# A fused attention and feed-forward layer on one core: half of two chunks' attention spreads issued by GpSimd, one score half added in pairs on VectorE, a second norm without scaled row sums, and a new instruction order

## The chip, the cores and the metric

The kernel runs on one core of a Trainium2 chip. The metric is the device time of one execution in microseconds (us); lower is better. Engine names are those of the profile: PE is TensorE (matmuls), PEld its weight loads, DVE is VectorE, ACT is ScalarE, POOL is GpSimd, SP is SyncE, which here only issues transfers (DMAs). A name with a q at its end (SPq, ACTq, POOLq) is the instruction stream of that engine that issues transfers.

## The reference

Input x has 2048 rows of 512 in bf16. One layer is computed: a norm, sliding attention, a residual, a second norm, a gated feed-forward part, a second residual.

```python
x = A_x
h = x + A(layernorm(x), wqkv, wo)
h2 = h + B(layernorm(h), W_gate, W_up, W_down)

# A: 32 heads of 16; each position looks at 8 keys, 2 apart, backwards
idx = pos[:, None] - arange(8) * 2
logits = einsum("bhsd,bhswd->bhsw", q, k[idx]) * 16 ** -0.5   # masked where idx < 0
o = einsum("bhsw,bhswd->bhsd", softmax(logits), v[idx])       # then o @ wo

# B: 512 -> 1376 -> 512
out = (relu(x @ W_gate) * (x @ W_up)) @ W_down
```

## The kernel before, in words

The 2048 rows are worked on in four chunks of 512, numbered 0 to 3. In a chunk:

1. **Norm and projections.** DVE takes the statistics of x (L469, L472), ACT or DVE centres and scales it (L514, L517), PE or a transposing DMA turns it (L546, L535). Twelve groups of four matmuls make q, k and v (L587; chunk 0's are cut in short pieces that follow the first weights and rows as they come), and ACT copies each from its PSUM bank (L595).
2. **Scores.** The eight keys of a position are two halves of four. For each half, DVE multiplies q by four shifted views of k: two products of 128x4096 for two pairs of feature groups (L638; for chunk 0 four products of 128x2048, L653). PE sums the features of each head by sixteen matmuls with a 0/1 matrix `sel` (L644). For the chunk halves in a list `PRE`, DVE first adds the two products (L682), and PE has only eight matmuls (L689). ACT takes the exponential (L703), and chunk 0's is masked by DVE (L706).
3. **Softmax and spread.** The two halves are added (L735), PE sums over the keys (L720), ACT makes the reciprocal (L726, L729), and DVE multiplies (L747; for chunk 0 only at the end, L802). Each half of the weights is then spread by four DMAs over the 16 features of each head (L763, `big<-ex` in the profile, 128 KB each). A table `BCD` has a letter for each of the four: S for SP's queue, P for POOL's.
4. **Weighted sum.** DVE multiplies the spread weights by v (L795; chunk 0 L810), and the eight products are added: the first step, eight to four, mostly by an accumulating DMA from POOL (L838, 512 KB), the rest by DVE (L798, L802, L832).
5. **Output projection and residual.** PE multiplies by wo, four groups of four matmuls (L876). DVE adds x and sums each row (L887).
6. **Second norm.** DVE multiplies each row sum by -1/512 (L452). ACT takes the sum of squares of x less the mean (L458). DVE centres x (L512). The rows aren't scaled here; the inverse variance is applied to the output of the feed-forward part.
7. **Feed-forward.** Pairs of 128 columns: PE makes up and gate (L949; the last 96 columns L916), ACT evacuates them (L953, L956) into two buffers each, DVE multiplies (L977, L926). Then PE multiplies by W_down (L1000), in groups of the first eight and the last three column blocks.
8. **Output.** DVE scales and adds the residual (L1008; chunks 0 and 1 by ACT and an accumulating DMA, L1006, L1029), and a DMA writes it (L1014, L1032). The last row block of chunk 3 is cut in pieces of 256, 128 and 128 columns.

Nothing fixes the order but a planner: the steps are gathered as operations, and a table of ranks, `RANK`, one number for each in the order of gathering, says in which order they are given out. Each engine then works through its own stream in that order and waits where an input, or a buffer to write to, isn't there. PE has eight PSUM banks; the 4096-wide tiles have six places (`big`, one of them the space of wqk_sb when its weights are done with). Ahead of the plan stands `setup`, which issues the first loads from SP's and ACT's queues, in a fixed order.

Of the kernel before, what the change touches and what calls it, by code (L numbers as in the profile page):

```python
# [8 lines left out]
P = 128  # L9
BF16 = mybir.dt.bfloat16  # L10
F32 = mybir.dt.float32
I32 = mybir.dt.int32
ACT = mybir.ActivationFunctionType
ALU = mybir.AluOpType
# [187 lines left out]
def kernel(  # L202
# [19 lines left out]
    DIL = 2  # L222
    PADL = 16
    DEN1 = (0, 1, 2, 3)
    BCD = {(0,0):"SSSS",(0,1):"SSSS",(1,0):"SSSS",(1,1):"SSSS",(2,0):"SSSS",(2,1):"SSSS",(3,0):"SSSS",(3,1):"SSSS"}
    PRE = ((3,0),(3,1))
    PRD = ()
    ODA = (0, 1)
# [861 lines left out]
```

## Time and profile before

| what | us |
|---|---|
| time, median of 3 runs | 192.63 (192.53 to 192.71) |
| the profiled execution, its time | 193.22 |
| its span, from the first to the last instruction | 191.3 |
| PE busy | 185.3 |
| DVE busy | 149.6 |
| ACT busy | 115.2 |
| POOL busy | 18.5 |

The span is the part of the profiled execution that the trace shows. The rest of its time, 1.9 us, lies around it. The profiled execution is 0.59 us longer than the median of the three runs. The mean granted clock of TensorE was 0.997.

In rows by time, the first number is the start, the second the length, and an idle time with what ended it stands in square brackets. In rows by group there is after the bar the busy time, the mean length of one in ns, and the idle time ahead of them. In rows of DMA issues the last number is the median time from issue to landing. Instructions of a group overlap at their ends, so that the step from one to the next is shorter than their length.

### The profile page before, as it was taken

To read this page: it belongs to the slowest core of one execution; us is meant where nothing else is said; L and a number is where in the kernel's file an instruction comes from. 1 tells how busy PE (TensorE), PEld (TensorE's weight loads), DVE (VectorE), ACT (ScalarE), POOL (GpSimd) and SP (SyncE) were. 2 spreads that over 40 slices of the span, in tenths; PEclk is the share of its full clock that TensorE was granted. 3 is DMA by queue.
4 is the path that set the end of the run, shared out by engine and by line. 5 is a ranking of instruction groups with operands and counts; after the bars stand their busy time and mean duration, and the time that the engine had idled before them with its cause. 6 is when DMAs were issued, how large, how long until landed. Compare 5 with 4: busy or idle time off the path is not lost.

```text
span 191.3 us, 3033 instructions
## 1 busy us (share of the span) xinstructions
PE 185.3 (97%) x1101; PEld 96.5 (50%) x1120; DVE 149.6 (78%) x246; ACT 115.2 (60%) x236; POOL 18.5 (10%) x34
## 2 busy tenths in 40 slices
PE   7899999999999999999999999999999999999993
PEld 7795555544455444644445544444446444445452
DVE  6899999999999999999999987999627503212632
ACT  2589999976748967753454875144855528517500
POOL 3000002500000042000055000042100000000000
PEclk9999999999999999999999999999999999999998
DMA  5998464992068589993479916779900460120302
GB/s 159 331 351 327 102 157 84 200 196 45 0 258 228 168 154 193 183 279 61 88 131 186 203 33 139 164 151 186 211 4 0 82 165 0 31 82 0 82 25 88
DMA packets 26718, 26.44 MB, mean 138 GB/s; under 512 B 12528, under 2 KB 22608, under 8 KB 26704
## 3 DMA queue, kind: packets, MB, share of 16 engines
q1 hardware_dynamic: 23248, 16.39, 30.9%
q0 software_dynamic: 2736, 8.91, 25.1%
q10 hardware_dynamic: 720, 0.95, 1.5%
q8 instruction: 9, 0.15, 0.3%
q14 instruction: 5, 0.04, 0.1%
HBM read 8.42 MB, written 2.10 MB: 55 GB/s over the span
## 4 chain that ended last, share of the span: by engine, by line
PE 94%; DMA 3%; issue 1%; ACTq 0%; DVE 0%
PE bank L949 36%; PE bank L587 22%; PE bank L1000 20%; PE bank L876 7%; DMA wqk_sb<-in_A_wqkv_dram 3%; PE bank L644 3%; PE bank L916 3%; PE bank L546 2%; PE bank L689 1%; PE bank L720 0%; ACTq L324 0%; ACTq L322 0%; DVE row L1008 0%
## 5 line engine op out<-in xcount | busy, mean ns | idle before, releaser
L949 PE MATMUL bank<-quad,wgu_sb 128*128 128x512 bf16 x311 | 72.1, 379 | 0.4
L949 PEld LDWEIGHTS <-wgu_sb 128*128 128x128 bf16 x320 | 30.9, 98 | 36.9 <-issue 1.7
L1000 PE MATMUL bank<-wd_sb,gT 128*128 128x512 bf16 (+3 forms) x195 | 39.6, 355 | 0.2
L956 ACT ACTIVATE gr<-bank 128x512 bf16<-128x512 f32 x40 | 23.2, 607 | 17.0 <-PE bank L949 13.0
L977 DVE TENSOR_TENSOR gT<-gr,up_sb 128x1024 bf16<-128x1024 bf16 x20 | 13.7, 688 | 23.5 <-ACT up_sb L953 20.3
L587 PE MATMUL bank<-quad,wqk_sb 128*128 128x512 bf16 (+2 forms) x171 | 30.0, 319 | 1.0 <-DMA wqk_sb<-in_A_wqkv_dram 0.7
L953 ACT CAST up_sb<-bank 128x512 bf16<-128x512 f32 x40 | 22.6, 594 | 10.5 <-PE bank L949 8.5
L1000 PEld LDWEIGHTS <-gT 128*128 128x128 bf16 (+1 forms) x198 | 18.5, 98 | 19.9
L638 DVE TENSOR_TENSOR big<-quad,kT 128x4096 bf16<-128x4096 bf16 x11 | 24.9, 2283 | 0.0
L587 PEld LDWEIGHTS <-wqk_sb 128*128 128x128 bf16 x176 | 16.9, 114 | 11.2 <-DMA wqk_sb<-in_A_wqkv_dram 0.9
L795 DVE TENSOR_TENSOR big<-big,vT 128x4096 bf16<-128x4096 bf16 x9 | 20.2, 2282 | 0.0
L458 ACT ACTIVATE junk<-x_sm,mv 128x512 bf16<-128x512 bf16 x16 | 11.7, 730 | 10.0 <-DVE mv L452 9.9
L587 PE MATMUL bank<-quad,wv_sb 128*128 128x512 bf16 x63 | 15.6, 379 | 0.1
L876 PE MATMUL bank<-wo_sb,quad 128*128 128x512 bf16 x63 | 15.2, 379 | 0.1
L838 POOL DMA_DIRECT2D big<-big x12 | 11.2, 1018 | 38.5 <-PE bank L587 29.4
L887 DVE SCALAR_TENSOR_TENSOR x_sm<-x_sm,bank 128x512 bf16<-128x512 bf16 x16 | 10.5, 680 | 3.7 <-PE bank L876 3.7
L798 DVE TENSOR_TENSOR big<-big 128x1024 bf16<-128x1024 bf16 (+2 forms) x18 | 11.5, 655 | 0.1
L1008 DVE SCALAR_TENSOR_TENSOR row<-bank,iv,x_sm 128x512 bf16<-128x512 f32 (+2 forms) x10 | 6.2, 640 | 6.8 <-PE bank L1000 6.8
L469 DVE BATCH_NORM_STATS2 st<-x_sm 128x6 f32<-128x512 bf16 x16 | 10.3, 681 | 1.2 <-DMA x_sm<-in_A_x_dram 1.2
L595 ACT CAST kT<-bank 128x512 bf16<-128x512 f32 x16 | 9.1, 592 | 2.8 <-DVE big L638 2.8
L595 ACT CAST quad<-bank 128x512 bf16<-128x512 f32 x16 | 9.4, 596 | 2.1 <-PE bank L587 1.9
L595 ACT CAST vT<-bank 128x512 bf16<-128x512 f32 x16 | 9.4, 596 | 2.0 <-PE bank L587 2.0
(79 smaller groups left out, 173.7 us busy)
## 6 DMA issues: line engine op xcount, KB each, us to landing
big<-big POOLq DMA_DIRECT2D x12, 512.0 KB, 5.7
big<-ex SPq DMA_DIRECT2D x32, 128.0 KB, 2.7
wqk_sb<-wqk_sb POOLq DMA_DIRECT2D x3, 512.0 KB, 4.5
wgu_sb<-in_B_W_gate_dram SPq DMA_DIRECT2D x1, 1376.0 KB, 11.2
wgu_sb<-in_B_W_up_dram SPq DMA_DIRECT2D x2, 688.0 KB, 4.7
wd_sb<-in_B_W_down_dram SPq DMA_DIRECT2D x2, 640.0 KB, 5.2
x_sm<-in_A_x_dram SPq DMA_DIRECT2D x2, 512.0 KB, 7.2
x_sm<-up_sb POOLq DMA_DIRECT2D x4, 256.0 KB, 5.1
```

What stands on the lines that cost most here:

```text
L458: nc.scalar.activation(out=junk[:, j % 2, :], in_=h.t[:] if h else x_sm[:, tk * BPC + j, :], func=ACT.Square, bias=mv.t[:, j, 0:1], scale= ...
L587: nc.tensor.matmul(mm.t[:, lo:hi], lhsT=wv_sb[:, dt, t:D:NT] if c == 2 else wqk_sb[:, dt, c * D + t:(c + 1) * D:NT], rhs=xnT.t[:, dt, lo:h ...
L595: nc.scalar.copy(out=o, in_=mm.t[:])
L638: V.tensor_tensor(out=pb.t[:].rearrange("p (t w) s -> p t w s", t=2), in0=q4, in1=k4, op=ALU.mult)
L795: V.tensor_tensor(out=mt.t[:], in0=ab.t[:], in1=v8, op=ALU.mult)
L798: V.tensor_tensor(out=mt.t[:, 0:n, :], in0=mt.t[:, 0:n, :], in1=mt.t[:, n:2 * n, :], op=ALU.add)
L876: nc.tensor.matmul(od.t[:], lhsT=OT.t[:, t, j * P:(j + 1) * P], rhs=wo_sb[:, t, :], start=(t == 0), stop=(t == NT - 1 and tk not in RPE))
L949: nc.tensor.matmul(mm.t[:fs, lo:hi], lhsT=wgu_sb[:, dt, g, ft * P: ft * P + fs], rhs=hnT.t[:, dt, lo:hi], start=(dt == 0), stop=(dt == NT ...
L953: nc.scalar.copy(out=ub.t[:fs, i, :], in_=um.t[:fs, :])
L956: nc.scalar.activation(out=gr.t[:fs, i, :], in_=gm.t[:fs, :], func=ACT.Relu)
L977: V.tensor_tensor(out=gt.t[:fs, 0:n, :], in0=gr.t[:fs, 0:n, :], in1=ub.t[:fs, 0:n, :], op=ALU.mult)
L1000: nc.tensor.matmul(od.t[:, c0:c1], lhsT=gts[ft].t[:fs, ft % 2, j * P:(j + 1) * P], rhs=wd_sb[:fs, ft, c0:c1], start=(ft == 0), stop=(ft == ...
```

## The change

There are five parts.

- **Spreads.** `BCD` for chunks 0 and 1 goes from "SSSS" to "SSPP": the first two of the four DMAs of each half stay with SP, the last two go to POOL.
- **Scores.** `PRE` gains (2,1): the second half of chunk 2 has its two products added by one 128x4096 addition on DVE, and 8 matmuls in place of 16.
- **Second norm.** The row sums aren't multiplied by -1/512. ACT squares 512 x less the sum instead (the small constant inside the logarithm grows by 512 squared), and DVE's centring becomes 512 x less the sum: two operations in one instruction, with a number and the row sum as operands. The common factor of 512 goes out with the inverse variance.
- **Numbers of the planner.** Estimated durations and latencies are changed. They issue nothing; they set which places and banks are taken.
- **Order.** `RANK` is a new table, so that instructions of all engines stand in other places.

```diff
-                    late = 3.0 if at < free.get("DT", -1.0) + 0.8 else 0.0
+                    late = 3.0 if at < free.get("DT", -1.0) - 0.5 else 0.0
...
-    BCD = {(0,0):"SSSS",(0,1):"SSSS",(1,0):"SSSS",(1,1):"SSSS",(2,0):"SSSS",(2,1):"SSSS",(3,0):"SSSS",(3,1):"SSSS"}
-    PRE = ((3,0),(3,1))
+    BCD = {(0,0):"SSPP",(0,1):"SSPP",(1,0):"SSPP",(1,1):"SSPP",(2,0):"SSSS",(2,1):"SSSS",(3,0):"SSSS",(3,1):"SSSS"}
+    PRE = ((2,1),(3,0),(3,1))
...
-                    def f_nm(j=j):
-                        V.tensor_scalar(out=mv.t[:, j, 0:1], in0=sm.t[:, j:j + 1], scalar1=-1.0 / D,
-                                        scalar2=None, op0=ALU.mult)
...
-                                             bias=mv.t[:, j, 0:1], scale=1.0, accum_out=sq.t[:, j:j + 1])
+                                             bias=sm.t[:, j:j + 1], scale=-float(D), accum_out=sq.t[:, j:j + 1])
...
-                    V.tensor_scalar(out=xn.t[:], in0=x, scalar1=mv.t[:, j, 0:1], scalar2=None, op0=ALU.add)
+                    V.tensor_scalar(out=xn.t[:], in0=x, scalar1=float(D), scalar2=sm.t[:, j:j + 1], op0=ALU.mult, op1=ALU.subtract)
...
-    MM, TP = 0.2165, 0.057
+    MM, TP = 0.2158, 0.056
```

Three places of the order are shown, each before and then now.

**POOL's stream, from the end of the setup on.** `ex` is a half of the softmax weights, `big` a 4096-wide tile; x2 is two instructions. Before, chunk 0's four accumulations stand first, then chunk 1's:

```order
L338 MEMSET wqk_sb 1x1
L838 DMA big_89<-big_89 128x2048
L838 DMA big_88<-big_88 128x2048
L838 DMA big_90<-big_90 128x2048
L838 DMA big_91<-big_91 128x2048
L838 DMA wqk_sb<-wqk_sb 128x2048
```

Now:

```order
L340 MEMSET wqk_sb 1x1
L767 DMA big_92<-ex_100 128x1x512 x2
L767 DMA big_92<-ex_101 128x1x512 x2
L842 DMA big_88<-big_88 128x2048
L842 DMA big_90<-big_90 128x2048
L842 DMA big_89<-big_89 128x2048
L842 DMA big_91<-big_91 128x2048
L767 DMA big_91<-ex_100 128x1x512 x2
L767 DMA big_91<-ex_102 128x1x512 x2
L842 DMA big_89<-big_89 128x2048
```

Two spreads of each half stand ahead of the accumulations of their chunk; in chunk 1 the second half (ex_100) comes first.

**DVE's stream in the middle, from the last products of chunk 2 on.** L638 (now L635) is a product of q and k, L795 (L799) one of the spread weights and v of chunk 1, L977 (L981) a gate product of chunk 0. Before:

```order
L638 TENSOR_TENSOR big_91<-quad_87,kT 128x4096
L638 TENSOR_TENSOR big_89<-quad_87,kT 128x4096
L638 TENSOR_TENSOR big_92<-quad_87,kT 128x4096
L795 TENSOR_TENSOR wqk_sb<-big_88,vT 128x4096
L795 TENSOR_TENSOR big_90<-big_88,vT 128x4096
L795 TENSOR_TENSOR big_91<-big_88,vT 128x4096
L977 TENSOR_TENSOR gT_93<-gr_111,up_sb_109 128x1024
```

Now:

```order
L635 TENSOR_TENSOR big_89<-quad_87,kT 128x4096
L635 TENSOR_TENSOR big_88<-quad_87,kT 128x4096
L635 TENSOR_TENSOR big_90<-quad_87,kT 128x4096
L799 TENSOR_TENSOR wqk_sb<-big_91,vT 128x4096
L799 TENSOR_TENSOR big_89<-big_91,vT 128x4096
L679 TENSOR_TENSOR big_92<-big_92,big_88 128x4096
L799 TENSOR_TENSOR big_90<-big_91,vT 128x4096
L981 TENSOR_TENSOR gT_93<-gr_112,up_sb_109 128x1024
```

The new addition (L679) stands among the products of chunk 1, ahead of the first gate product.

**DVE's stream at the very end.** These are the outputs of chunk 3, each from a PSUM bank to a row buffer. Before:

```order
L1008 SCALAR_TENSOR_TENSOR row_104<-bank_138,iv_136,x_sm 128x256
L1008 SCALAR_TENSOR_TENSOR row_108<-bank_141,iv_136,x_sm 128x512
L1008 SCALAR_TENSOR_TENSOR row_105<-bank_144,iv_136,x_sm 128x512
L1008 SCALAR_TENSOR_TENSOR row_106<-bank_143,iv_136,x_sm 128x512
L1008 SCALAR_TENSOR_TENSOR row_104<-bank_140,iv_136,x_sm 128x128
L1008 SCALAR_TENSOR_TENSOR row_104<-bank_139,iv_136,x_sm 128x128
```

Now:

```order
L1012 SCALAR_TENSOR_TENSOR row_108<-bank_141,iv_136,x_sm 128x512
L1012 SCALAR_TENSOR_TENSOR row_104<-bank_142,iv_136,x_sm 128x128
L1012 SCALAR_TENSOR_TENSOR row_106<-bank_139,iv_136,x_sm 128x512
L1012 SCALAR_TENSOR_TENSOR row_105<-bank_144,iv_136,x_sm 128x512
L1012 SCALAR_TENSOR_TENSOR row_104<-bank_140,iv_136,x_sm 128x256
L1012 SCALAR_TENSOR_TENSOR row_104<-bank_145,iv_136,x_sm 128x128
```

The piece of 256 columns moved from the first place to the last but one, and the last piece is now the one that ACT's queue writes out (columns 384 to 512); before it was the one ahead of it, which SP's queue writes.

More of the change, by code (lines that the diff above doesn't have):

```diff
@@ L445, in layernorm @@
         for grp in groups:
-            ag, nms = [], {}
+            ag = []
             gk = str(grp[0]) if len(groups) > 1 else ""
@@ L459, in f_sq @@
                                              func=ACT.Square,
-                                             bias=mv.t[:, j, 0:1], scale=1.0, accum_out=sq.t[:, j:j + 1])
-                    a = nms[j] = add((ln + "nm" + gk, tk), "DVE", DSM, f_nm, [src[j][0]], pr, take=[mv], use=[sm], lat=DL)
-                    ag.append(add((ln + "sq" + gk, tk), "ACT", 0.66 if h else 0.72, f_sq, [a], pr,
-                                  take=[sq], use=[mv] + ([h] if h else []), lat=AL))
+                                             bias=sm.t[:, j:j + 1], scale=-float(D), accum_out=sq.t[:, j:j + 1])
+                    ag.append(add((ln + "sq" + gk, tk), "ACT", 0.66 if h else 0.72, f_sq, [src[j][0]], pr,
+                                  take=[sq], use=[sm] + ([h] if h else []), lat=AL))
                 else:
@@ L522, in norm @@
                 f = lambda: f_xn(j, xn)
-                d, u = ([nms[j]], [mv]) if residual else ([e], [nb, rs] if on_act else [mv, rs])
+                d, u = ([src[j][0]], [sm]) if residual else ([e], [nb, rs] if on_act else [mv, rs])
                 if on_act:
                     return xn, add((ln + "xn" + gk, tk), "ACT", AX, f, d, pr, take=[xn], use=u, lat=AL)
-                return xn, add((ln + "xn" + gk, tk), "DVE", DXN, f, d, pr, take=[xn], use=u, lat=DL)
+                return xn, add((ln + "xn" + gk, tk), "DVE", 0.27 if residual else DXN, f, d, pr, take=[xn], use=u, lat=DL)
             step = 1 if tk == 0 and not residual else 2
@@ L684, with f_pb, f_sc @@
                 a = add(("pa%d" % hf, tk), "DVE", D40, f_pa, [a for a, _, _ in prd], apr, use=[b for _, b, _ in prd], lat=DL)
-                def f_sc(sc=sc, pb=prd[0][1]):
-                    for u in range(2):
+                nu = 2
+                if (tk, hf) in PRE2:
+                    def f_pb(p0=prd[0][1]):
+                        V.tensor_tensor(out=p0.t[:, 0:4, :], in0=p0.t[:, 0:4, :], in1=p0.t[:, 4:8, :], op=ALU.add)
+                    a = add(("pb%d" % hf, tk), "DVE", D20, f_pb, [a], apr, use=[prd[0][1]], lat=DL)
+                    nu = 1
+                def f_sc(sc=sc, pb=prd[0][1], nu=nu):
+                    for u in range(nu):
                         for g in range(4):
@@ L894 @@
             else:
-                a = add(("rs%d" % j, tk), "DVE", 0.63, f_rs, [a], base + 50, take=[sm], use=[od], lat=DL)
+                a = add(("rs%d" % j, tk), "DVE", 0.613, f_rs, [a], base + 50, take=[sm], use=[od], lat=DL)
             hd.append((a, od))
@@ L1043 @@
         if o.dq and o.eng in ("SP", "ACT"):
-            o.hw = 4 if n[:2] == "bd" else 2 if n == "ldd" and o.dur > 0.5 else 1
+            o.hw = round(o.dur / 0.7) if n[:2] == "bd" else 2 if n == "ldd" and o.dur > 0.5 else 1
         if n in ("qe1", "qe5"):
```

44 lines of the change are left out of this document (23 added, 21 removed), and 74 rows, old and new, of the table RANK.

## The prediction

> **What bounds the kernel now.** I read the page's busy shares and slices first.
>
> ```profile
> PE 185.3 (97%) x1101; PEld 96.5 (50%) x1120; DVE 149.6 (78%) x246; ACT 115.2 (60%) x236; POOL 18.5 (10%) x34
> ...
> PE   7899999999999999999999999999999999999993
> ...
> DVE  6899999999999999999999987999627503212632
> ...
> PE 94%; DMA 3%; issue 1%; ACTq 0%; DVE 0%
> ```
>
> PE is at 9 in every slice from the third to the last but one, and the last row, the chain by engine, is PE for 94%. DVE is at 9 too but for two slices, though only up to the 28th (about 134 us). The windows view says how full that is.
>
> ```profile
> 12.00:62.00 50.00, 49.58 (x330) 26.42 (x335) 49.83 (x79) 41.34 (x76) 3.62 (x4) 1.00 0.65 169
> 62.00:112.00 50.00, 49.74 (x268) 23.43 (x273) 49.15 (x57) 31.62 (x69) 8.70 (x10) 1.00 0.77 161
> 112.00:150.00 38.00, 37.79 (x184) 17.96 (x186) 29.80 (x60) 20.96 (x46) 4.33 (x5) 1.00 0.54 109
> ```
>
> The third column is PE, the fifth DVE. PE lacks 0.4 us in the first 50 and 0.3 us in the next, at a granted clock of 1.00. DVE lacks 0.2 and 0.9 us. So PE sets the end, and DVE runs beside it with almost no room until 112 us. The chain of waits then gives PE's two ends.
>
> ```profile
> 1.67 6.42 DMA wqk_sb<-in_A_wqkv_dram
> ...
> 8.14 0.81 PE bank L587 x11
> ...
> 49.75 0.98 PE bank L644 x16
> ...
> 95.38 0.55 PE bank L689 x8
> ...
> 180.15 8.03 PE bank L1000 x58
> ...
> 188.20 0.35 DVE row L1008
> ```
>
> From 8.14 to 188.18 us PE is without a break: 180.04 us of matmuls. Ahead of it lies the load of wqk_sb, behind it one DVE output and its transfer to 191.3 us. A change here pays only what it takes from these 180.04 us or from the ends; anything that comes late to PE is added.
>
> **What the change takes from PE.** The second score group of chunk 2 goes from 16 matmuls to 8, because the two products are added first. The chain has both forms: 0.98 us for 16 (L644) and 0.55 us for 8 (L689, chunk 3). Gain 0.43 us, in full on the path. No other PE work is removed; everything else is moved.
>
> **What it puts on DVE.** One 4096-wide add is new; sixteen tiny multiplications go; the sixteen centring instructions become two-operation ones.
>
> ```profile
> 91.92 2.28 DVE L682 TENSOR_TENSOR big<-big,wqk_sb 128x4096 bf16<-128x4096 bf16 x1
> 94.12 4.49 DVE L795 TENSOR_TENSOR big<-big,vT 128x4096 bf16<-128x4096 bf16 x2
> ...
> 55.47 0.32 DVE L452 TENSOR_SCALAR mv<-sm 128x1 f32<-128x1 f32 x4
> 55.72 0.41 DVE L747 TENSOR_TENSOR ex<-ex,rec 128x512 bf16<-128x512 bf16 x1
> ...
> L512 DVE TENSOR_SCALAR row<-x_sm,mv 128x512 bf16<-128x512 bf16 x16 | 5.1, 348 | 0.3
> L517 DVE TENSOR_SCALAR row<-x_sm,mv,rs 128x512 bf16<-128x512 bf16 x4 | 1.5, 402 | 0.0
> ```
>
> The add holds DVE from 91.92 to 94.12: 2.20 us. Four row sums take 0.25 us, so sixteen give back 1.0. The new centring is not in the trace. Its bounds are 0 (it costs as L512) and 16 x 0.054 = 0.9 us (as L517, the nearest two-operation row, though with both operands per row); I take 0.4. DVE's net is +1.6 us, of which +2.2 comes at once in chunk 2. Whether that costs anything is read at the places where PE takes what DVE makes.
>
> ```profile
> 49.76 0.76 DVE L802 TENSOR_TENSOR quad<-big,rec 128x512 bf16<-128x512 bf16 x2
> 50.66 2.77 PE L876 MATMUL bank<-wo_sb,quad 128*128 128x512 bf16 x12
> ...
> 84.54 0.69 DVE L977 TENSOR_TENSOR gT<-gr,up_sb 128x1024 bf16<-128x1024 bf16 x1
> 85.70 1.03 PE L1000 MATMUL bank<-wd_sb,gT 128*128 128x512 bf16 x4
> ```
>
> *Chunk 0's output projection.* Before, DVE ends its last input at 50.52 and PE starts at 50.66: 0.14 us to spare. In the new order one 4096-wide product of chunk 1 stands behind these instructions instead of ahead: 50.52 - 2.20 = 48.32. PE has a score group (0.98) and, net, one projection of four matmuls (0.86) less ahead: 50.66 - 1.84 = 48.82. To spare: 0.50 us.
>
> *Chunk 0's down projection.* Before, the last of the first four gate products ends at 85.23 and PE starts at 85.70. In the new order DVE has the add (+2.20) and, less, a product (2.20), nine small attention and residual steps (3.8) and four row sums (0.25) ahead: about 81.1. PE has the 0.43 us and the sixteen projection matmuls of chunk 1 (3.45) less ahead: 81.8. To spare: 0.7 us. So 2.2 us more on DVE cost nothing here as long as DVE meets no new wait; with over 0.7 us of waits, PE pays the rest.
>
> Later the spare time is larger: after 112 us DVE lacks 8 us of 38. The saved waits for row sums on ACT move no PE instruction.
>
> **The spreads.** Four transfers a half on SP become two on SP and two on POOL, in chunks 0 and 1.
>
> ```profile
> 19.96 0.16 DVE L706 TENSOR_TENSOR ex<-ex,mask 128x16 bf16<-128x16 bf16 x1
> 20.15 6.21 SPq L763 DMA_DIRECT2D big<-ex  x8
> ...
> 26.49 1.20 DVE L810 TENSOR_TENSOR big<-big,vT 128x2048 bf16<-128x2048 bf16 x1
> ...
> 36.13 1.75 POOL L838 DMA_DIRECT2D big<-big  x2 [1.14 <-DVE big L810]
> ...
> 95.74 0.86 POOL L1029 DMA_DIRECT2D x_sm<-up_sb  x1 [20.73 <-ACT up_sb L1006]
> ...
> big<-ex SPq DMA_DIRECT2D x32, 128.0 KB, 2.7
> ...
> x_sm<-up_sb POOLq DMA_DIRECT2D x1, 256.0 KB, 3.4
> ...
> big<-big POOLq DMA_DIRECT2D x1, 512.0 KB, 4.6
> ...
> big<-big POOLq DMA_DIRECT2D x12, 512.0 KB, 5.7
> ...
> big<-big POOLq DMA_DIRECT2D x2, 512.0 KB, 8.2
> ```
>
> POOL issues one in 0.88 us and has nothing else to do until the first accumulation. A 128 KB transfer from POOL is not in the trace. The quickest rows are 3.4 us for 256 KB and 4.6 for 512 KB, so by a straight line 2.8 for 128 KB; the slowest is 8.2. Bounds 2.7 (SP's) and 8.2; I take 2.8, since the issues stand alone as in the 3.4 row. In chunk 0 the first mask now comes one product later: 21.1. POOL's second spread is issued at 22.1 and lands at 24.9; the first multiplication is at 26.49 + 0.49 = 26.98 (a sum of two rows and two aggregations moved ahead). Two us to spare. Chunk 1 is tighter: both halves are normalised by 57.0, POOL's fourth spread is issued at 59.7 and lands at 62.5, and the multiplication is due at 63.8. There 1.3 us are to spare on DVE, and 0.7 more before PE notices: a landing time over 4.8 us is the point from which it costs. The weight loads that follow SP's spreads now start beside POOL's last ones; 128 KB against 640 KB, so I add nothing. I price this edit at nothing.
>
> **The two ends.** Weights first:
>
> ```profile
> 3.74 0.33 SPq L339 DMA_DIRECT2D wqk_sb<-in_A_wqkv_dram  x1
> ...
> wqk_sb<-in_A_wqkv_dram SPq DMA_DIRECT2D x1, 256.0 KB, 5.7
> ...
> 9.46 6.30 PE L587 MATMUL bank<-quad,wqk_sb 128*128 128x128 bf16 x63
> ...
> 188.01 0.36 ACTq L1014 DMA_DIRECT2D out_dram<-row  x1
> 188.58 0.33 SPq L1014 DMA_DIRECT2D out_dram<-row  x1
> ...
> out_dram<-row ACTq DMA_DIRECT2D x1, 32.0 KB, 1.6
> ...
> out_dram<-row SPq DMA_DIRECT2D x1, 32.0 KB, 1.4
> ```
>
> The last quarter of wqk_sb lands at 9.44. Before, PE first used it three short matmuls into the row at 9.46, about 9.65; the new order has four short matmuls less ahead of it, some 0.06 us each by the eleven from 8.14 on, and comes to it at about 9.42. Cost 0 to 0.1; I take 0.05. At the end the last quarter row now goes out from ACT's queue, which took 1.6 us, where SP's took 1.4: 0 to 0.2, I take 0.1. The 64 KB piece is issued half a microsecond ahead of it.
>
> **Sum.** -0.43 + 0.05 + 0.10 = -0.28 us. The profiled execution took 193.22 us (span 191.3), so it would take 192.94; against the median of the runs, 192.63, that is **192.35 us**, with 192.2 to 192.5 from the bounds of the two ends.
>
> **Rivals.** (1) *All of it is kept.* Neither end costs and the shorter SP queue helps a little: 192.0 to 192.2. For it: both prices are at the edge of what the rows resolve. (2) *Spent in small waits.* Spare times of 0.5 and 0.7 us are met by a bank or an evacuation that is late by as much again: 192.5 to 193.0. For it: DVE is over 98% busy up to 112 us, and the gate products have two buffers to each of their inputs. Against: before, 0.14 us were to spare at the first projection and PE still ran through. (3) *POOL's spreads come late, slower.* The place is chunk 1's multiplication at 63.8 us, the point 4.8 us of landing time. At 5.7 us, what a 512 KB accumulation mostly takes, PE loses 0.9: 193.25. At 8.2 it loses 3.4: 195.7. Another way to the same place is that POOL can't issue while a DVE product runs: then the four issues at 57.0 get in at the products' ends, 2.20 us apart, the last at 63.6, and land at 66.4; DVE waits 2.6, PE 1.9: 194.3. Against it: the issue at 95.74 lies inside two DVE products that run back to back from 94.12 to 98.5 and took the usual 0.86 us, and its data landed in 3.4.
>
> The Trainium skill has that way as a rule ("SBUF — State Buffer", section "SBUF: two separate sides"): descriptors of a transfer issued from GpSimd are written by its cores, which VectorE locks out while it runs in a two-port mode; it advises SP's or ACT's queue. By that rule the change would cost the 1.9 us; by the row at 95.74 nothing, and I go by the row.
>
> **How the numbers follow.** Forecast 0.45; rival 1 0.20; rival 2 0.13; rival 3 0.22. A measurement of this kernel tells about 0.2% from no change, that is 0.385 us: faster is below 192.245. Rival 1 gives faster all its 0.20, the low edge of the forecast 0.13: 0.33. Slower is above 193.015: rival 3, 0.22. The rest, 0.45, is the same. The range goes from 191.9, the low end of rival 1 less the 0.1 us by which runs differ, to 193.7, so that about half of rival 3 is left out above. The likeliest case's own range is 192.2 to 192.5.
>
> **What would show it.** In the changed profile, right: PE without a break from about 8.14 to 187.8; 8 matmuls on L693 at about 72 us with 0.55 in the chain; POOL's spreads landing within 3.5 us; no DVE wait named after a DMA at 27 or 64 us. Wrong: a PE wait at the first projection of chunk 0 (about 48.8) or its down projection (about 81.8), with DVE late ahead of it; POOL issues stretched beyond 1 us; or a last transfer that lands later than 189.8.

## The result and the profile after

The changed kernel takes **193.9 us** (median of 11 runs, 192.67 to 195.5), beside 192.91 for the kernel before (11 runs, 192.53 to 193.54): ratio **1.005** with an interval of 1.0027 to 1.0072. It is 0.5% slower; 192.35 was forecast. The profiled execution of the changed kernel took 194.02 us, its span is 192.2 (before: 193.22 and 191.3). A few runs of a kernel are over 1.5% longer than its fastest one, and the ratios leave them out; of the twelve with all spreads on SP, below, these are three, the profiled execution among them.

Line numbers of the changed kernel are a few higher: spreads L767, products L635, additions of products L679, their matmuls L693, multiplications by v L799 (chunk 0: L814), W_down's matmuls L1004, W_down's loads L309 and L312. In kernels with an edit of their own they are a few higher again.

The page of the changed kernel: busy times, the slices of PE and DVE, and the chain by engine.

```profile
PE 185.3 (96%) x1093; PEld 96.4 (50%) x1112; DVE 149.9 (78%) x231; ACT 115.6 (60%) x236; POOL 22.9 (12%) x43
...
PE   7999999999999989989999999999999999999994
...
DVE  6999999999999599999999997799726902120624
...
PE 80%; DVE 9%; DMA 6%; issue 2%; SPq 1%; ACT 1%; DVEq 0%
```

PE is busy for as long as before, but it has two slices with an 8 now (the 15th and the 18th, 67 to 72 and 82 to 86 us), and DVE has a 5 in the 14th (62 to 67 us). PE's share of the chain fell from 94% to 80%: something else holds the end up in the middle of the program. The chain, in order of time, says where.

```profile
56.29 1.73 PE bank L584 x8
...
58.94 6.62 DMA wd_sb<-in_B_W_down_dram
...
65.90 2.01 issue
67.90 2.28 DVE big L799
70.19 2.20 DVE big L679
72.39 2.20 DVE big L799
...
75.19 2.20 DVE big L799
...
78.33 2.20 DVE big L635
...
83.00 3.63 PE bank L1004 x16
```

The chain leaves PE at 58.5 us, runs through transfers until 65.6, then through DVE, and is back on PE at 83 us, chunk 0's down projection. The rows of DVE around 64 us and of PE behind it:

```profile
61.22 2.28 DVE L635 TENSOR_TENSOR big<-quad,kT 128x4096 bf16<-128x4096 bf16 x1
65.69 2.29 DVE L799 TENSOR_TENSOR wqk_sb<-big,vT 128x4096 bf16<-128x4096 bf16 x1 [2.19 <-DMA wd_sb<-in_B_W_down_dram]
```

```profile
72.44 0.61 PE L693 MATMUL bank<-big,sel 128*32 128x512 bf16 x8 [0.81 <-DVE big L679]
...
83.00 3.63 PE L1004 MATMUL bank<-wd_sb,gT 128*128 128x512 bf16 x16 [0.53 <-DVE gT L981]
...
97.13 8.79 PE L953 MATMUL bank<-quad,wgu_sb 128*128 128x512 bf16 x39 [0.45 <-issue]
```

DVE stands for 2.19 us ahead of chunk 1's first multiplication. PE then waits 0.81 us for the new addition, 0.53 for a gate product and 0.45 at 97 us: 1.79 us in all, and before it had none of these. The first two come of VectorE's delay; whether the third does is taken up below.

What DVE waits for is named after a load of W_down, which it does not read. The issues and landings of chunk 1's spreads and of the loads settle that. First SP's rows of issues before the change:

```profile
56.21 5.12 SPq L763 DMA_DIRECT2D big<-ex  x8
61.38 0.59 SPq L308 DMA_DIRECT2D wd_sb<-in_B_W_down_dram  x1
```

Then those of the changed kernel, SP's, POOL's, and landings (each from a stretch that holds one issue).

```profile
56.38 2.51 SPq L767 DMA_DIRECT2D big<-ex  x4
58.94 2.17 SPq L309 DMA_DIRECT2D wd_sb<-in_B_W_down_dram  x2
```

```profile
57.23 2.23 POOL L767 DMA_DIRECT2D big<-ex  x4 [20.05 <-DVE row L509]
```

```profile
big<-ex SPq DMA_DIRECT2D x1, 128.0 KB, 6.5
...
big<-ex POOLq DMA_DIRECT2D x1, 128.0 KB, 6.4
...
wd_sb<-in_B_W_down_dram SPq DMA_DIRECT2D x1, 640.0 KB, 8.2
```

SP's last spread is issued at 58.3 and lands 6.5 us later, at 64.8; POOL's last is issued at 58.9 and lands 6.4 us later, at 65.2. Before, the last spread, issued at 60.8, landed after 2.7 us, at 63.4, and the multiplication started at 64.04 without a wait. The first load of W_down, issued at 58.9, lands only at 67.1, behind the start of the multiplication at 65.69. So the name in the bracket is a neighbour: DVE waited for the spreads, and they were late. Two kernels below bear that out: there too the multiplication starts about 0.5 us after the last landing, at 63.57 after 63.1 and at 65.55 after 65.1, as here at 65.69 after 65.2.

How full the transfer engines were meanwhile is in the windows view, of DVE here; the last two numbers of a row are the mean busy share of the 16 DMA engines and GB/s. Before:

```profile
58.00:60.00 2.00, 2.00 (x2) 1.00 0.85 217
60.00:62.00 2.00, 2.00 (x2) 1.00 0.83 207
62.00:64.00 2.00, 2.00 (x1) 1.00 0.85 220
```

and in the changed kernel:

```profile
58.00:60.00 2.00, 2.00 (x2) 1.00 0.88 210
60.00:62.00 2.00, 2.00 (x2) 1.00 0.96 167
62.00:64.00 2.00, 1.50 (x1) 1.00 0.80 238
64.00:66.00 2.00, 0.31 (x1) 1.00 1.07 373
```

Before, eight spreads issued one by one over 5.1 us kept the 16 engines at 0.83 to 0.85 in the first two rows; the last row holds the load too, issued at 61.38. In the changed kernel the two queues had issued all eight in 3.1 us, and the loads, 1376 KB, came behind them from 58.94 on, 2.4 us earlier than the one load before. The share went up to 0.96, and between 60 and 62 us fewer bytes moved, not more.

### The profile page after: what moved, and what is told of

It is laid out like the page before. It is cut to its first block, busy times and chain, and to the rows that moved or that the text cites. A ratio compares the mean times of both kernels' runs of the same rounds, so it can differ in the third digit from the quotient of the medians.

```text
span 192.2 us, 3016 instructions
## 1 busy us (share of the span) xinstructions
PE 185.3 (96%) x1093; PEld 96.4 (50%) x1112; DVE 149.9 (78%) x231; ACT 115.6 (60%) x236; POOL 22.9 (12%) x43
## 4 chain that ended last, share of the span: by engine, by line
PE 80%; DVE 9%; DMA 6%; issue 2%; SPq 1%; ACT 1%; DVEq 0%
PE bank L953 27%; PE bank L584 20%; PE bank L1004 20%; PE bank L880 7%; DVE big L799 3%; DMA wd_sb<-in_B_W_down_dram 3%; DMA x_sm<-in_A_x_dram 3%; PE bank L920 2%; PE bank L543 2%; PE bank L641 2%; DVE big L635 1%; DVE big L679 1%; DVE gT L981 1%; PE bank L693 1%; ACT quad L559 1%
## 5 line engine op out<-in xcount | busy, mean ns | idle before, releaser
L953 PE MATMUL bank<-quad,wgu_sb 128*128 128x512 bf16 x311 | 71.1, 379 | 0.9 <-issue 0.4
L1004 PE MATMUL bank<-wd_sb,gT 128*128 128x512 bf16 (+3 forms) x195 | 39.3, 355 | 0.7 <-DVE gT L981 0.5
L960 ACT ACTIVATE gr<-bank 128x512 bf16<-128x512 f32 x40 | 23.7, 606 | 18.5 <-PE bank L953 17.4
L1004 PEld LDWEIGHTS <-gT 128*128 128x128 bf16 (+1 forms) x198 | 18.4, 98 | 20.4 <-DVE gT L981 1.0
L981 DVE TENSOR_TENSOR gT<-gr,up_sb 128x1024 bf16<-128x1024 bf16 x20 | 13.6, 687 | 17.9 <-ACT gr L960 9.9
L635 DVE TENSOR_TENSOR big<-quad,kT 128x4096 bf16<-128x4096 bf16 x12 | 27.1, 2282 | 0.0
L456 ACT ACTIVATE junk<-x_sm,sm 128x512 bf16<-128x512 bf16 x16 | 11.6, 725 | 14.1 <-DVE x_sm L891 14.1
L880 PE MATMUL bank<-wo_sb,quad 128*128 128x512 bf16 x63 | 14.6, 379 | 0.1
L799 DVE TENSOR_TENSOR big<-big,vT 128x4096 bf16<-128x4096 bf16 x6 | 13.5, 2282 | 0.0
L802 DVE TENSOR_TENSOR big<-big 128x1024 bf16<-128x1024 bf16 (+2 forms) x19 | 12.0, 655 | 0.4 <-DMA big<-big 0.4
L584 PEld LDWEIGHTS <-wv_sb 128*128 128x128 bf16 x64 | 7.1, 113 | 6.3 <-issue 0.4
```

Of the source, the lines that this page charges most:

```text
L456: nc.scalar.activation(out=junk[:, j % 2, :], in_=h.t[:] if h else x_sm[:, tk * BPC + j, :], func=ACT.Square, bias=sm.t[:, j:j + 1], scale ...
L584: nc.tensor.matmul(mm.t[:, lo:hi], lhsT=wv_sb[:, dt, t:D:NT] if c == 2 else wqk_sb[:, dt, c * D + t:(c + 1) * D:NT], rhs=xnT.t[:, dt, lo:h ...
L635: V.tensor_tensor(out=pb.t[:].rearrange("p (t w) s -> p t w s", t=2), in0=q4, in1=k4, op=ALU.mult)
L799: V.tensor_tensor(out=mt.t[:], in0=ab.t[:], in1=v8, op=ALU.mult)
L802: V.tensor_tensor(out=mt.t[:, 0:n, :], in0=mt.t[:, 0:n, :], in1=mt.t[:, n:2 * n, :], op=ALU.add)
L880: nc.tensor.matmul(od.t[:], lhsT=OT.t[:, t, j * P:(j + 1) * P], rhs=wo_sb[:, t, :], start=(t == 0), stop=(t == NT - 1 and tk not in RPE))
```

## The experiments

**Theory L:** the spreads are late because W_down's loads, which stand behind SP's spreads, are now issued while the spreads are in flight; VectorE's delay reaches PE. **Rivals:** GpSimd's spreads are slow by themselves (G); eight spreads fill the transfer engines whoever issues them, so that a faster issue gains nothing (D); the new order is at fault whatever the spreads do; the new addition is what PE can't afford. Each ratio is to runs of the kernel before on the same chip (medians 192.75 to 192.94, 23 to 35 runs). First the five kernels about the spreads and the loads.

### The loads held back

```diff
         if n == "d":
             lo, hi = (0, 5) if i == 0 else (5, NFF)
+            if i == 0:
+                nc.gpsimd.tensor_copy(out=wd_sb[0:1, 0:8, 0:1], in_=ab1[0].t[0:1, :, 0:1])
...
         if tk == 1 and "d" in LATE:
+            ab1.append(ab)
```

A copy of 8 elements on GpSimd, from chunk 1's spread tile into the place that the loads then overwrite, makes them wait until the spreads have landed. Nothing else is changed.

> The kernel after, and the two W_down loads wait until all eight spreads of chunk 1 have landed (a GpSimd copy of eight elements, from the spread tile into the weights' tile, stands ahead of them). Theory L (the loads, issued right behind SP's spreads, take DMA time from the last spreads): the last spread lands by 63.2 us instead of 65.3, DVE waits under 0.4 us ahead of chunk 1's multiplication instead of 2.2, PE's waits at 72, 83 and 97 us are gone (1.8 us), the ratio to the kernel before is 0.996 to 0.999. Rival G (transfers issued by GpSimd land late by themselves): DVE still waits 1.5 us or more, ratio 1.003 to 1.006. Rival D (eight spreads fill the DMA engines whoever issues them, and a doubled issue rate gains nothing): they land at 63 to 64, DVE waits 0 to 1 us, ratio 0.998 to 1.001.

Measured: 192.54 us (12 runs), ratio 0.999 (0.9974 to 1.0007); once more, in a later comparison, 192.65, ratio 1.0001 (0.9978 to 1.0023). The loss is gone. VectorE's, GpSimd's and SyncE's rows of this kernel:

```profile
63.57 2.29 DVE L803 TENSOR_TENSOR wqk_sb<-big,vT 128x4096 bf16<-128x4096 bf16 x1 [0.41 <-issue]
```

```profile
56.89 2.23 POOL L771 DMA_DIRECT2D big<-ex  x4 [20.35 <-DVE row L513]
63.41 0.21 POOL L312 COPY wd_sb<-big 1x8 bf16<-1x8 bf16 x1 [4.29 <-DMA big<-ex]
```

```profile
56.04 2.51 SPq L771 DMA_DIRECT2D big<-ex  x4
63.65 0.94 SPq L313 DMA_DIRECT2D wd_sb<-in_B_W_down_dram  x2
```

The spreads are issued as in the changed kernel, half of them by GpSimd, and the copy that waits for them starts at 63.41. GpSimd's last spread, issued at 58.5, lands after 4.6 us, at 63.1. The multiplication waits 0.41 us and not 2.19, and PE's waits at 72 and 83 us are gone. So GpSimd's spreads are not slow enough by themselves to cost anything; with the loads out of the way eight spreads take 7.1 us from the first issue, where in the changed kernel they took 8.8 (56.4 to 65.2). Before, with one queue and the load behind them, they took 7.2 (56.2 to 63.4): the faster issue gains nothing, as rival D has it. Theory L and D hold together.

The two waits come to 1.34 us. Each less its own before, the changed kernel and the gated one differ by 1.2 us (+0.99 and -0.23), in the second comparison by 1.1. The wait of 0.45 at 97 us is another matter: it stands in this profile too, with 0.50 at 95 us, and not in the second profile of the same kernel.

### All spreads on SP again

```diff
-                    ws = [w for w in range(4) if BCD[tk, hf][w] == eng[0]]
+                    ws = [w for w in range(4) if BCD[tk, hf][w] == let]
+                    if let == "P" and tk in (0, 1):
+                        eng, q = "SP", nc.sync
```

> The kernel after, with all spreads of chunks 0 and 1 issued by SP, in the new order; everything else as after. Theories L and G both: SP issues the eight of chunk 1 from 56.4 to 61.3 us, the loads follow as they did before the change, the last spread lands near 63.5, DVE waits under 0.3 us, ratio 0.996 to 0.999. Were the loss in the new order or in the addition on DVE and not in the spreads, the ratio would stay at 1.003 to 1.006.

Measured: 194.1 us, ratio 1.0067 (1.0038 to 1.0096): a miss, and close to the 1.003 to 1.006 that a fault of the new order or of the addition would have given. The next kernel, with chunk 1's spreads alone on SP, has no such loss, so this one lies in chunk 0. The profiled execution (197.49 us) took 3.4 us more than the median, so its wait is a likely place only, and its size is not that of the others:

```profile
35.95 4.44 PE L584 MATMUL bank<-quad,wqk_sb 128*128 128x512 bf16 x11 [3.19 <-DMA quad<-row]
```

SP now issues eight spreads of chunk 0 for 5.99 us from 20.47, and the four transposes of a later chunk's rows behind them start at 26.56, not 25.65. The fourth is issued at 30.6 and lands after 5.2 us (2.4 in the changed kernel, by the median of its sixteen), beside the first accumulation, which GpSimd issues at 30.48. PE waits for it at 36 us. So the new order counts on the half that GpSimd takes in chunk 0, where the shorter queue of SP is worth something; that it is worth it by these transposes is not shown.

### Chunk 1's spreads on SP, chunk 0's shared

The same edit for chunk 1 alone:

```diff
-                    if let == "P" and tk in (0, 1):
+                    if let == "P" and tk in (1,):
                         eng, q = "SP", nc.sync
```

> The kernel after, with chunk 1's spreads all on SP again, chunk 0's still half on GpSimd. If only chunk 1's place costs (theories L and G): as the run with all on SP, within 0.1%, ratio 0.996 to 0.999. If chunk 0's half costs too: longer than that run by 0.2% or more, with a DVE wait at about 27 us.

Measured: 192.77 us, ratio 1.000 (0.998 to 1.002). The issues of chunk 1 in this kernel:

```profile
56.14 5.11 SPq L769 DMA_DIRECT2D big<-ex  x8
```

The loads start behind them, at 61.30, and the multiplication waits 0.56 us. With one queue the spreads' own issue time, 5.1 us, holds the loads back as well as the copy does. This and the gate remove the same loss with GpSimd's part in chunk 1 once kept and once not: it is not GpSimd's issue that costs.

### The spreads shared in the order of before

```diff
-    BCD = {(0,0):"SSSS",(0,1):"SSSS",(1,0):"SSSS",(1,1):"SSSS",...
+    BCD = {(0,0):"SSPP",(0,1):"SSPP",(1,0):"SSPP",(1,1):"SSPP",...
```

The kernel before with that part alone (GpSimd's issues stand in the order right behind SP's).

> The kernel before with its own order and norm, and only the last two of the four spreads of each half of chunks 0 and 1 issued by GpSimd. SP is through with its half by 58.8 us, so one W_down load (640 KB) follows there at once, where after has two. Theory L: the last spread lands 0.5 to 1.5 us later than its 63.4, DVE waits as long, little of it is covered at the first down projection, ratio 1.001 to 1.005. Rival G: the same or more, up to 1.008. Rival D: no change, 0.999 to 1.001.

Measured: 192.69 us, ratio 0.999 (0.9968 to 1.0011). Theory L gave 1.001 to 1.005 here: a miss; rival D's 0.999 to 1.001 came. SP's rows, and VectorE's:

```profile
55.30 3.01 SPq L764 DMA_DIRECT2D big<-ex  x4
58.36 0.76 SPq L309 DMA_DIRECT2D wd_sb<-in_B_W_down_dram  x1
```

```profile
63.15 2.27 DVE L797 TENSOR_TENSOR wqk_sb<-big,vT 128x4096 bf16<-128x4096 bf16 x1
```

One load follows SP's spreads at once, at 58.36, and the multiplication has no wait: SP's last spread, issued at 57.3, lands after 4.8 us and GpSimd's, issued at 57.4, after 4.5, so that all eight are there at 62.1, 6.8 us after the first issue. So the shared issue neither gains nor costs in the order of before. It couldn't gain, since VectorE came to the multiplication only at 63.15. And here a load beside the spreads did not make them late, though the transfer engines were at 1.00 and 1.03 of their time from 56 to 60 us (with the end of an earlier load, which landed at 57.9, and the start of this one).

### Only the second load held back

The gate stands ahead of the second load; the first is issued behind SP's spreads as in the changed kernel. The edit is shown against the kernel with all loads held back:

```diff
-            if i == 0:
-                nc.gpsimd.tensor_copy(out=wd_sb[0:1, 0:8, 0:1], in_=ab1[0].t[0:1, :, 0:1])
+            if i == 1:
+                nc.gpsimd.tensor_copy(out=wd_sb[0:1, 5:7, 0:4], in_=ab1[0].t[0:1, :, 0:1].rearrange(...))
```

> The kernel after, with only the second of the two 640 KB W_down loads (and the 96-row rest) waiting for chunk 1's spreads; the first still follows SP's spreads at once. Theory L by amount (what lies on the DMA engines besides the spreads decides): between after and the run with both loads gated; the last spread lands about 64 us, DVE waits 0.6 to 1.4 us, ratio 0.999 to 1.002. If one load is as bad as two: DVE waits 1.8 us or more, ratio 1.003 to 1.006.

Measured: 194.2 us (6 runs), ratio 1.0066 (1.0047 to 1.0085), not between the changed kernel and the gated one. Its rows of VectorE and PE:

```profile
65.55 2.29 DVE L803 TENSOR_TENSOR wqk_sb<-big,vT 128x4096 bf16<-128x4096 bf16 x1 [1.54 <-DMA wd_sb<-in_B_W_down_dram]
```

```profile
72.30 0.62 PE L697 MATMUL bank<-big,sel 128*32 128x512 bf16 x8 [0.17 <-DVE big L683]
...
82.86 3.63 PE L1009 MATMUL bank<-wd_sb,gT 128*128 128x512 bf16 x16 [0.53 <-DVE gT L986]
...
97.28 8.79 PE L958 MATMUL bank<-quad,wgu_sb 128*128 128x512 bf16 x40 [0.74 <-issue]
```

In the profile the amount does count: VectorE waits 1.54 us where it waited 2.19 with three loads and 0.41 with none, and up to 83 us PE has lost 0.70, not 1.34. At 97 us it loses more, 0.74, so that the sum is 1.44 against 1.79, and the times can't be told apart. One load of 640 KB is enough for most of the loss: the eight spreads take 8.2 us from the first issue (56.9 to 65.1). Why the same load costs nothing in the order of before is open. There VectorE came to the multiplication 7.85 us after the first issue, here after 7.13, but that covers only half of it, since the spreads themselves landed sooner, after 6.8 us. The rows show one more difference: there both queues were through with the spreads (58.0 and 58.3) when the load was issued at 58.36; here, as in the changed kernel, GpSimd issued its last one (59.4 to 60.0) beside the load (59.44). No run tests which of these it is.

### The norm alone

The kernel before with the norm part alone: no scaled row sums, centring in two operations (the line of the centring is shown).

```diff
-                    V.tensor_scalar(out=xn.t[:], in0=x, scalar1=mv.t[:, j, 0:1], scalar2=None, op0=ALU.add)
+                    V.tensor_scalar(out=xn.t[:], in0=x, scalar1=float(D), scalar2=sm.t[:, j:j + 1], op0=ALU.mult, op1=ALU.subtract)
```

> The kernel before with the new second norm alone (no multiplication of the row sums, two-operation centring), same order. DVE saves 16 x 0.063 us and pays 16 x 0 to 0.054 us; neither is on PE's path. Ratio 0.999 to 1.001; the centring takes 348 to 402 ns in the groups.

Measured: 192.77 us, ratio 1.0004 (0.9989 to 1.002). The group of the centrings in this kernel:

```profile
L511 DVE TENSOR_SCALAR row<-x_sm,sm 128x512 bf16<-128x512 bf16 x16 | 4.9, 346 | 0.1
```

346 ns each, where the one-operation form took 348. The sixteen row sums fall away and nothing is paid for it, nor is anything gained.

### The addition alone

In this section and the next, theory W is that the addition's 2.2 us of VectorE cost TensorE waits, which eat the 0.43 us that the 8 matmuls fewer are worth; the rival is that they are gained.

```diff
-    PRE = ((3,0),(3,1))
+    PRE = ((2,1),(3,0),(3,1))
```

> The kernel before with one part of the change alone: the second half of chunk 2's q*k products is added in pairs on VectorE, right behind those products, so that TensorE does 8 matmuls there and not 16. Theory W (the addition's 2.2 us of VectorE reach a point that TensorE waits for, also in the order of before): no gain, ratio 0.9985 to 1.004, and the trace names a wait of TensorE on VectorE or on transposed rows behind 72 us that the kernel before does not have. Rival G (the order of before has the slack, so the 0.43 us are gained): ratio 0.996 to 0.9985, TensorE's unbroken run shorter by 0.4.

Measured: 195.03 us (6 runs), ratio 1.0129 (1.0091 to 1.0168), far above what theory W gave.

```profile
56.67 2.28 DVE L639 TENSOR_TENSOR big<-quad,kT 128x4096 bf16<-128x4096 bf16 x1
58.98 2.29 DVE L683 TENSOR_TENSOR big<-big,big 128x4096 bf16<-128x4096 bf16 x1
```

```profile
61.33 0.62 PE L691 MATMUL bank<-big,sel 128*32 128x512 bf16 x8 [1.62 <-DVE big L683]
...
83.43 3.63 PE L878 MATMUL bank<-wo_sb,quad 128*128 128x512 bf16 x16 [0.43 <-ACT gr L958]
```

In the order of before PE reads these products right behind the second one. The addition puts 2.2 us between them, PE waits 1.62 us for it, and the 0.43 us of matmuls are small against that. In the new order the group stands at 72 us, eleven us later, with feed-forward matmuls ahead of it. So order and addition are one edit: the addition needs that order. The two waits less the 0.43 make 1.6 us, and by that much the span is longer (medians 192.5 and 190.9). The median time is 2.3 above before's: the other 0.7 lies outside the span, which leaves 1.8 to 3.3 us around it in the six runs of this kernel and mostly 1.8 to 1.9 elsewhere. What takes that time is not explained.

### With and without the addition, 16 or 8 matmuls

All on the kernel with the loads held back. Without the addition, chunk 2's second score group has its 16 matmuls again:

```diff
+            elif (tk, hf) == (2, 1):
+                a = add(("pa%d" % hf, tk), "DVE", 0.0, None, [a for a, _, _ in prd], apr, lat=0.0)
+                scd = [add(("sc%d" % hf, tk), "PE", 4 * MM + SW, lambda p=prd: [f() for _, _, f in p], ...
```

> As the run with both loads gated, and without the new addition: chunk 2's second half has its 16 score matmuls again (0.98 us instead of 0.55), and DVE has 2.20 us less. If the 0.43 us on PE is a clear gain: 0.43 us (0.2%) longer than the gated run. Theory W (the addition makes DVE late to chunk 1's second norm, and PE's wait of 0.5 us at 95 us for the transposed rows eats the gain): that wait falls under 0.15 us, and the time is within 0.1% of the gated run's.

Measured: 192.2 us (12 runs), ratio 0.9967 (0.9949 to 0.9985). Both kernels were then run again side by side.

> The gated kernel (chunk 1's W_down loads held until the spreads have landed) with the new addition, once more, beside the same without it on one chip. Theory W (addition eats its gain): ratio 0.998 to 1.000, not below the one without the addition. Rival (addition gains 0.43 us, and the first comparison was scatter): 0.2% below the one without it.

> The gated kernel without the new addition, once more, beside the same with it on one chip. Theory W: ratio 0.995 to 0.998, at or below the one with the addition. Rival: 0.2% above the one with the addition.

Measured: 192.65 with the addition, 192.31 without it, ratios 1.0001 (0.9978 to 1.0023) and 0.9974 (0.9953 to 0.9995). Twice the kernel without the addition is 0.34 us faster. The second time most of that lies outside the span (190.6 with the addition, 190.55 without). The other way to hold the loads back, chunk 1's spreads on SP, was run without the addition too (both edits as above):

> The changed kernel with chunk 1's spreads all issued by SyncE and without the new addition (16 score matmuls in chunk 2's second half, as before); no gate on the weight loads. Theory (what lost time was that the weight loads were issued beside spreads, and what ate the 0.43 is the addition): the loads start near 61.3 behind SyncE's eight spreads, VectorE waits at most 0.7 us at 64, TensorE has no wait behind 10 us, ratio 0.995 to 0.998, as with the gate and without the addition. Rival (the addition costs nothing, its 0.43 is a gain): slower than the same kernel with the addition by 0.43 us, ratio 1.001 to 1.003.

Measured: 192.59 us, ratio 1.000 (0.9973 to 1.0026), with no wait of PE over 0.12 us behind 7 us in its profile. By its median it lies between theory and rival, and by its interval it decides nothing.

Two kernels complete the square, and both compute other scores in that one group: one adds and then keeps 16 matmuls, one neither adds nor reads the second products.

```diff
-                def f_sc(sc=sc, pb=prd[0][1], nu=nu):
+                def f_sc(sc=sc, pb=prd[0][1], nu=2 * nu if tk == 2 else nu):
...
-                                             rhs=pb.t[:, 4 * u + g, :], start=(u == 0),
+                                             rhs=pb.t[:, 4 * (u % 2) + g, :], start=(u == 0),
```

> The gated kernel with the addition, but chunk 2's second score group keeps 16 matmuls (the added half is read twice, so this group's scores are not the reference's). Against the gated kernel only TensorE's 8 matmuls, 0.43 us, come back. Theory W (the addition's 2.2 us of VectorE cost TensorE waits, and the 8 matmuls are worth their 0.43): 192.8 to 193.1, ratio 1.000 to 1.002; the 2.2 us alone then cost 0.6 to 0.8 against the gated kernel without the addition (192.2 and 192.31). Rival (VectorE's 2.2 us are free): the same as the gated kernel without the addition, 192.2 to 192.4, ratio 0.997.

```diff
-                a = add(("pa%d" % hf, tk), "DVE", D40, f_pa, ...
+                a = add(("pa%d" % hf, tk), "DVE", 0.0 if tk == 2 else D40, None if tk == 2 else f_pa, ...
```

> The gated kernel with the 8 matmuls but without the addition in front of them (the second products of that half are left out of the scores). Theory W: the 0.43 of TensorE are gained in full, 191.8 to 191.9, ratio 0.994 to 0.996. Rival (the 8 matmuls are not on the path, TensorE's time is used up elsewhere): no faster than with 16, 192.2 to 192.4, ratio 0.997.

| medians, us, less the median of before on the same chip | with the addition | without it |
|---|---|---|
| 16 matmuls | -0.10 (192.84) | -0.55, -0.44 (192.20, 192.31) |
| 8 matmuls | -0.23, -0.10 (192.54, 192.65) | -0.71 (192.23) |

Across a row the addition costs 0.4 with 16 matmuls and 0.55 with 8. Down a column 8 matmuls fewer are worth 0.07 and 0.2, not 0.43. Each median is uncertain by about 0.4 us (the intervals of the ratios are 0.2% to either side), so the cost of the addition, seen three times, is likely and its size is not; by the spans of the same runs it is 0.3 and 0.5. The worth of the matmuls is not told from nothing nor from 0.43. PE in these profiles:

```profile
95.25 8.79 PE L958 MATMUL bank<-quad,wgu_sb 128*128 128x512 bf16 x39 [0.50 <-issue]
```

```profile
95.48 8.79 PE L958 MATMUL bank<-quad,wgu_sb 128*128 128x512 bf16 x40 [0.18 <-issue]
```

The first row is of the gated kernel's first profile, the second of the kernel with addition and 16 matmuls. PE waits there for chunk 1's turned rows. The transposes that bring them are issued from 87.81 on in the first of these, behind centrings that stand behind the projection's residual on VectorE. The three profiles without the addition (two with the gate, one with chunk 1's spreads on SP) have no wait of PE behind 9 us but the 0.12 us at 22 us that nearly all profiles in the new order have, nor has the one with neither addition nor second products. But the gated kernel's second profile has none at 95 us either, so the place is likely, and not shown to be the whole 0.4.

### The kernel before, once more

> The kernel before once more, for a second profile of it: how far the start of PE's unbroken run (8.14 us in the first profile) depends on when the first weights land. If it starts near 7.2 us here, as in the profiles of the changed kernels, the first profile had a late start and the comparison of spans with it flatters the changed kernels by up to 0.9 us.

Measured: 193.28 us, span 191.4. Its first pause is in another place than in the first profile of before:

```profile
7.82 0.81 PE L587 MATMUL bank<-quad,wqk_sb 128*128 128x128 bf16 x11 [0.18 <-DMA wqk_sb<-in_A_wqkv_dram]
```

0.18 us for the weights, where it was 0.69. The other profiles have from nothing to 1.7 us of waits ahead of 8.3 us, on rows of x or on weights, with the same loads. So single profiles differ by more than a microsecond at the start, and from one profile a gain of that size can't be read.

The matmuls themselves can be compared over all of them: from the first projection matmul to the last matmul of the program, less the waits over 0.15 us named behind it.

| | PE's run less named waits, us | median |
|---|---|---|
| 16 matmuls in the group, 8 profiles | 179.98, 180.10, 180.25, 180.44, 180.44, 180.45, 180.46, 180.57 | 180.44 |
| 8 matmuls, 7 profiles | 179.78, 179.83, 179.85, 180.03, 180.11, 180.27, 180.37 | 180.03 |

The difference of the medians is 0.41, as the matmuls alone would give; the two groups overlap. (The profile with all spreads on SP is left out.)

## Why the prediction was wrong, step by step

1. **PE's 0.43 us: right as work, wrong as time.** The run of PE is shorter by 0.41 in the median. But "in full on the path" did not hold: in the changed kernel three waits of 1.79 us stand against it, and with the loads held back the addition likely still costs what it saves.
2. **VectorE's terms: right but for one.** The addition takes 2.20 us as priced. The new centring takes 349 ns in the changed kernel where 348 were before: 0.0, and not the 0.4 taken; the low end of its bounds was right.
3. **The spare times at the two junctions: right.** The rows of the changed kernel, VectorE's and PE's:

```profile
47.11 0.75 DVE L806 TENSOR_TENSOR quad<-big,rec 128x512 bf16<-128x512 bf16 x2
...
82.26 0.68 DVE L981 TENSOR_TENSOR gT<-gr,up_sb 128x1024 bf16<-128x1024 bf16 x1
```

```profile
48.32 2.75 PE L880 MATMUL bank<-wo_sb,quad 128*128 128x512 bf16 x12
```

At chunk 0's output projection VectorE ends at 47.86 and PE starts at 48.32 without a wait: 0.46 us to spare, 0.50 foretold. At the down projection, less the waits before it, VectorE would be there at 82.94 - 2.19 = 80.75 and PE at 83.00 - 0.53 - 0.81 = 81.66: 0.9 to spare, 0.7 foretold (81.1 and 81.8). The prediction said that with over 0.7 us of waits PE pays the rest, 1.5 of 2.19 us: it paid 0.81 and 0.53 up to there, 1.34.
4. **The spreads "priced at nothing": this step failed.** "The weight loads that follow SP's spreads now start beside POOL's last ones; 128 KB against 640 KB, so I add nothing." That sentence saw the meeting and set its price at nothing by comparing sizes. The last spread took 6.4 us from issue to landing and not 2.8. The point from which it costs was put at 4.8; by the rows of the changed kernel it was 5.0 (6.35 less the 1.34 that PE paid). With 6.4 us the prediction's own working gives 192.35 + 1.6 = 193.95, and 193.9 was measured. That they come so close is in part luck: PE paid 1.34 us for the spreads, and 0.45 at 97 us, a wait that the gated kernel can have too, is not in that working. That the loads are the cause the gated kernel shows: loads away, spreads at 63.1, the loss gone. The windows of before gave a warning, 0.83 to 0.85 from 58 to 62 us with little but the spreads in flight, which the step didn't look at. They don't settle it: with the spreads shared in the order of before the engines were fuller, and a load beside the spreads cost nothing. Why it does in the new order stays open.
5. **Rival 3 had the place and the price, with the wrong mechanism.** It made GpSimd slow, by itself or by VectorE's products, and had a chance of 0.22. GpSimd issued its four spreads in 2.23 us from 57.23 on, 0.56 each, while three of VectorE's products ran back to back from 56.82 to 63.51: it did not wait for them, as the row at 95.74 had already said. The prediction took the rule of the Trainium skill ("SBUF — State Buffer", section "SBUF: two separate sides") to foretell such a wait. It does not: the rule is for VectorE's two-port mode, and the same section, under "Who interferes with whom", says that a `tensor_tensor`, which these products are, has no two-port mode. With that the trace agrees.
6. **What two queues are worth.** The step assumed that an earlier issue is an earlier landing. Here it was not: the last of the eight spreads landed 7.1 us after the first issue with two queues (the gated kernel), and 7.2 with one (before). The Trainium skill says this too ("DMA: Bandwidth & Descriptors", section "Issuing engines are not separate DMA queues"): all queues end in the same 16 engines, and several issuers save only the time of issuing. These runs agree.
7. **The ends: not told from nothing.** The pause for the first weights varied more from run to run (0 to 0.7) than the 0.05 that was priced, so that no run shows this term. The last piece from ACT's queue took 1.5 us, as SP's did: 0.0, not 0.10.

The sum by what was measured: -0.41 for the matmuls, +1.79 for PE's waits, 0 for the rest: +1.4; the medians say +1.0. The 0.4 between them is of the size in which PE's runs differ between profiles.

**The version that beats both** is the new order with shared spreads, the loads held back, and no addition: 192.2 and 192.31 us in two comparisons, ratios 0.9967 and 0.9974, both intervals below 1.

## What to carry to other kernels

Price a transfer that moves earlier by how busy the transfer engines are in that stretch, not by its size beside its neighbour. At 0.83 to 0.85 the room was small: in two of the three kernels in which a load was issued before the first of the spreads had landed, the spreads came late by about a microsecond or more. In the third they did not, so the share is a warning and not a price; the price is found by holding the transfer back. A faster issue of urgent transfers also brings forward whatever stands behind them in the queue, so check that the next ones can wait, or make them wait. An operation that trades 0.43 us of the bounding engine for 2.2 us of one that is over 98% busy has to be tested in the order in which it will run: the same addition made the kernel 2.3 us longer in one order (1.6 of them in the span), and in the other it likely costs about 0.4, as much as it saves.

## What the chip did that was not expected

- **GpSimd's issue takes the larger part of the engines.** Between 59 and 62 us of the changed kernel the packets of its queue took 73% of the engines' time and SP's 21%, while loads and spreads of both queues were in flight; the gated kernel, with no loads, has 60% and 24%. The changed kernel's rows (packets, MB, share of the engines' time), q0 being GpSimd's queue:

```profile
q0 software_dynamic: 130, 0.37, 73.0%
q1 hardware_dynamic: 232, 0.21, 21.4%
```

- **SP's own last spread was late too**: 6.5 us for one that stood ahead of the loads in the same queue, beside 5.0 with no loads about. Which part of the path the loads and the spreads share, the runs don't tell.
- **A 128 KB spread from GpSimd is issued in 0.56 us** when four stand together, quicker than the 0.88 of its accumulations of 512 KB, and lands in 4.2 us with no loads about, beside 4.0 for SP's in the same stretch.
